# Linear attention into a Swish feed-forward layer: x of batches 1 and 2 transposed by DMA, loads issued behind it, num_mm of batch 2 earlier

## The chip, the cores and the metric

The kernel runs on one core of one Trainium2 chip. The metric is the device time of one launch in microseconds (us). The kernel before takes 293.0 us in the median of 13 runs (292.68 to 294.04). A core has a matmul engine (PE, with PEld for its weight loads), two engines for elementwise work (DVE and ACT), POOL (here mostly an issuer of loads), SP (here an issuer of stores and transposes) and 16 DMA engines[...].

## The reference, cut to what matters

```python
# q, k, v: [8 batches, 8 heads, 576 rows, 64]; w_in [512, 2048]; w_out [2048, 512]; beta [2048]
phi = lambda x: np.where(x > 0, x, np.exp(x) - 1.0) + 1.0
kv  = einsum('bhsd,bhse->bhde', phi(k), v)
num = einsum('bhsd,bhde->bhse', phi(q), kv)
den = einsum('bhsd,bhd->bhs', phi(q), phi(k).sum(axis=2)) + 1e-6
x   = (num / den).transpose(0, 2, 1, 3).reshape(4608, 512)
h   = x @ w_in
out = (h * sigmoid(beta * h)) @ w_out
```

## The kernel before, in words

The order on every engine is written by hand: instructions stand on each engine in the order in which the code calls them, and each waits for what it reads. Per batch of 576 rows there are four main tiles of 128 rows and a tail of 64; two tails together make one more tile, and the eight tails are handled as a ninth "batch" at the end.

A batch goes through these steps. `load_k`, `load_q` and `load_v` each issue two DMAs from POOL (L72 and L76), which turn float32 in memory into bf16 on chip. `exp_` (ACT, L229), `relu` (DVE, L237) and `phi` (DVE, L242) make phi of q and k; `v_copy` (DVE, L385) puts v beside columns of ones. `kv_mm` (PE, L362, 40 matmuls) and `kv_evac` (DVE, L372) make kv. q is transposed, in batch 1 by `q_trans` on PE (L395, with copies on ACT, L387), from batch 2 on by `q_trans_dma`, a DMA transpose on SP's queue (L407). `num_mm` (PE, L421, 4 matmuls a tile) and `num_norm` (DVE, L435 to L437) make a tile of x. x has to be transposed again to be the moving operand of the feed-forward layer. In batches 0 to 2 `x_trans` does that for the main tiles: 4 PE transposes (L455) and one copy on ACT or DVE (L385, L387). From batch 3 on, and for all tails, `num_norm` itself issues a DMA transpose on SP (L441); `by_dma` decides it with `DMA_T = 3`.

`h_phase` computes h by groups: a group is one block `ff` of 128 hidden units and a range of row tiles, 4 matmuls (L475) and one Silu on ACT (L467). `(ff, 0, 4)` is a full group, `(ff, 0, 2)` and `(ff, 2, 4)` are its halves, which can begin when only some tiles of x are there. `h_last` does the last four blocks of batches 0 and 1 in the PSUM buffer `att`, which has two slots. `y_phase_wide` (batches 0 and 1) runs over ff outside and the four tiles inside, and the last four ff tile by tile; `y_phase` (from batch 2 on) runs tile by tile. The matmuls of both are L527. `y_out` copies a result out (ACT L535 in the wide form, DVE L537 otherwise) and SP issues its store (L514 for batch 0, L519 for the others, L522 for the tails).

Attention of batch n+1 is threaded between the groups of batch n by a plan, a dictionary from group number to functions. The plan of `y_phase_wide` counts ff from 0 to 11 and then the four tiles as 12 to 15:

```python
y_phase_wide(1, {
    1: [F(phi, 2, 0), F(q_trans_dma, 2), F(phi, 2, 1)],
    6: [F(kv_mm, 2), F(kv_evac, 2), F(held_load, 4, 2)],
    11: [F(num_mm, 2, 0), F(num_norm, 2, 0)],
    12: [F(num_mm, 2, 1), F(num_norm, 2, 1), F(x_trans, 2, 0, wide=True, dve=True)],
```

Loads stand on POOL in the order k1, q1, w_out's third quarter (L111), v1, its fourth quarter, then k2, q2, v2, k3, q3, v3 without a wait for attention. `held_load` puts a one-element copy on POOL (`hold`, L598) that reads the end of a transposed q, so that all POOL issues behind it wait for that transpose.

Of the kernel before, what the change touches and what calls it, by code (L numbers as in the profile page):

```python
# [16 lines left out]
def kernel(  # L17
# [12 lines left out]
    B, H, S, D = q.shape  # L30
# [5 lines left out]
    NJ = 4  # L36
# [1 line left out]
    TAIL = S - MAIN  # L38
    NT = NJ + 1
    EA = D + 2  # L40
    DMA_T = 3
    TINY = 2.0 ** -30

    ctx.enter_context(tc.manual_schedule())
# [63 lines left out]
    def load_w_out(i):  # L108
        for ii in range(2):
            c0 = 4 * i + 2 * ii  # L110
            nc.gpsimd.dma_start(out=w_out_f[i][ii], in_=w_out_v[:, c0 : c0 + 2, :])  # L111
# [92 lines left out]
        nc.vector.tensor_add(beta_c, beta_s, beta_m)  # L204
        nc.vector.reciprocal(rbeta, beta_c)

    def w_out_scale(i, on_dve=4):
        for c in range(4):
            ff = 4 * i + c
            dst, src, by = w_out_sb[i][:, c, :], w_out_f[i][c // 2][:, c % 2, :], rbeta[:, ff : ff + 1]  # L210
            if c < on_dve:
                nc.vector.tensor_scalar(dst, src, by, None, ALU.mult)
            else:
                nc.scalar.activation(dst, src, ACTF.Copy, scale=by)  # L214
# [1 line left out]

    st = {}

    def by_dma(b):
        return b >= DMA_T  # L220

    def begin(b):
        st[b, "p"] = work.tile([P, 2, NT, DM], BF16, tag="qk_p", name="qk_p")
# [17 lines left out]
    def phi(b, a, h0=0, h1=H):  # L241
        nc.vector.tensor_tensor(  # L242
            st[b, "p"][:, a].rearrange("p j (h d) -> p h j d", h=H)[:, h0:h1],
            st[b, "r", a][:, h0:h1], st[b, "e", a][:, h0:h1], ALU.min,
        )
# [182 lines left out]
    def num_norm(b, t):  # L428
        n = P
        den = work.tile([P, 2, 4], F32, tag="den", name="den")  # L430
        rden = work.tile([P, 2, 4], F32, tag="rden", name="rden")
        xs = work.tile([P, 2, 4, D], BF16, tag="xs", name="xs", bufs=4)
        st[b, "xs", t] = xs
        nv = st[b, "n", t][:n, :, 0 : 4 * (D + 1)].rearrange("p a (h e) -> p a h e", h=4)
        nc.vector.tensor_scalar(den[:n], nv[:, :, :, D], 1e-6, None, ALU.add)  # L435
        nc.vector.reciprocal(rden[:n], den[:n])  # L436
        nc.vector.tensor_mul(  # L437
            xs[:n], nv[:, :, :, 0:D], rden[:n, :, :, None].to_broadcast([n, 2, 4, D])
        )
        if by_dma(b) or t == NJ:  # L440
            nc.sync.dma_start_transpose(  # L441
                out=x_dst(b, t), in_=xs.rearrange("p a h d -> p (a h d)")[:n]
            )
# [6 lines left out]
    def x_trans(b, t, wide=False, dve=False):  # L450
        n = P
        xv = st[b, "xs", t].rearrange("p a h d -> p (a h d)")
        tp = tr_bank(wide)[:, 0 : KC * P].rearrange("p (c n) -> p c n", c=KC)
        for p in range(KC):
            nc.tensor.matmul(  # L455
                tp[:, p, :n], xv[:n, p * P : (p + 1) * P], identity[:n, :n],
                is_transpose=True, start=True, stop=True, skip_group_check=True,
            )
        copy(x_dst(b, t), tp[:, :, :n], dve)
# [80 lines left out]
    def y_phase(b, plan):  # L540
        for t in range(4):
            if b == B and t == 3:
                y_end()
                return
            yp = mm_bank([P, DM])
            for ff in range(FC):
                y_mm(b, yp, t, ff)
                if ff % 4 == 3 and ff < FC - 1:
                    run(plan, 4 * t + ff // 4)
            y_out(b, t, yp)  # L550
            run(plan, 4 * t + 3)
# [33 lines left out]
    def load_next(b):
        if b < B:
            if b >= 5:
                load_v(b)
            load_k(b)
            load_q(b)  # L590
            if b < 5:
                load_v(b)

    held = consts.tile([1, 1], BF16)

    def hold(a):

        nc.gpsimd.tensor_copy(held, a)  # L598

    def held_load(b, n):  # L600

        hold(st[n, "qT"][0:1, NJ, KC - 1, 0:1])
        load_next(b)
# [12 lines left out]
    def F(f, *a, **k):  # L616
        return lambda: f(*a, **k)
# [31 lines left out]
    num_mm(0, 0)  # L649
    num_mm(0, 1)  # L650
    num_norm(0, 0)
    exp9(0, QF, N9)
    relu9(0, QF, N9)
    silu_table()
    warm(4)
    x_trans(0, 0, dve=True)
    num_norm(0, 1)
    phi9(0, QF, 6)
    phi9(0, 6, N9)
    qb2 = att_banks(BF16)  # L660


    load_w_out(2)
    load_v(1)
    load_w_out(3)

    def tidy():
# [3 lines left out]
    def q_rest():  # L671
        for t in range(2, NT):
            q_trans9(t, qb2, (t - 2) * 256)
        for t in range(2, NT):
# [5 lines left out]
        + [(ff, 0, 2) for ff in range(4, 8)] + [(ff, 2, 4) for ff in range(8)]  # L680
        + [(ff, 0, 4) for ff in range(8, 12)],
        {
            1: [F(x_trans, 0, 1)],
            3: [F(q_rest)],
            5: [F(num_mm, 0, 2), F(num_norm, 0, 2)],
            7: [F(num_mm, 0, 3), F(num_norm, 0, 3)],
# [5 lines left out]


    clear_tail(2)
    load_next(2)
    h_last(0, xT[0], [])
    begin(1)
    exp_(1, 1)
    exp_(1, 0)
    silu_table()  # L700
    relu(1, 1)
    relu(1, 0)
    w_out_scale(2)
    phi(1, 1)
    phi(1, 0)
    v_copy(1, 0, HH)
    v_copy(1, HH, H, dve=False)
    y_phase_wide(0, {
        4: [F(load_next, 3)],
        10: [  # L710
            F(q_trans, 1, 0, 1, 2, 3), F(kv_mm, 1), F(kv_evac, 1), F(w_out_scale, 3, 2),
        ],
        11: [F(num_mm, 1, 0), F(num_norm, 1, 0)],
        12: [F(num_mm, 1, 1), F(num_norm, 1, 1), F(x_trans, 1, 0, wide=True)],
        13: [F(num_mm, 1, 2), F(num_norm, 1, 2), F(x_trans, 1, 1, wide=True)],
        14: [F(num_mm, 1, 3), F(num_norm, 1, 3), F(q_trans, 1, 4)],
    })

    ALL = [(ff, 0, 4) for ff in range(FC)]
    h_phase(  # L720
        1, xT[1],
        [(ff, 0, 2) for ff in range(4)] + [(ff, 2, 4) for ff in range(4)] + ALL[4:12],
        {
            0: [F(x_trans, 1, 2), F(num_mm, 1, 4), F(num_norm, 1, 4)],
            1: [F(x_trans, 1, 3)],
            8: [F(begin, 2), F(relu, 2, 0)],
            10: [F(relu, 2, 1)],
            12: [F(v_copy, 2)],
        },
    )  # L730
    begin(3)
# [3 lines left out]
    silu_table()  # L735
    y_phase_wide(1, {
        1: [F(phi, 2, 0), F(q_trans_dma, 2), F(phi, 2, 1)],
        6: [F(kv_mm, 2), F(kv_evac, 2), F(held_load, 4, 2)],
        11: [F(num_mm, 2, 0), F(num_norm, 2, 0)],
        12: [F(num_mm, 2, 1), F(num_norm, 2, 1), F(x_trans, 2, 0, wide=True, dve=True)],  # L740
        13: [F(num_mm, 2, 2), F(num_norm, 2, 2)],
        14: [
            F(x_trans, 2, 1, wide=True, dve=True), F(num_mm, 2, 3), F(num_norm, 2, 3),
        ],
    })

# [61 lines left out]
```

## Time and profile before

| what | value |
|---|---|
| median of 13 runs | 293.0 us |
| the profiled execution's own time | 292.83 us |
| its span | 291.1 us |
| PE busy | 281.1 us |
| ACT busy | 173.4 us |
| DVE busy | 118.4 us |
| POOL busy | 50.9 us |
| first feed-forward matmul (L475) starts | 16.90 us |
| y_phase_wide of batch 0 starts | 33.33 us |
| h_phase of batch 1 starts | 51.53 us |
| h_last of batch 1 ends | 66.40 us |
| h_phase of batch 2 starts | 83.07 us |
| h_phase of batch 3 starts | 113.44 us |

Times in the profile count from the start of the span. The span is 1.73 us shorter than the profiled execution's time. The rows of stage starts come from the chain of work that ended last.

### The profile page before, as it was taken

To read this page: it belongs to the slowest core of one execution; us is meant where nothing else is said; L and a number is where in the kernel's file an instruction comes from. 1 tells how busy PE (TensorE), PEld (TensorE's weight loads), DVE (VectorE), ACT (ScalarE), POOL (GpSimd) and SP (SyncE) were. 2 spreads that over 40 slices of the span, in tenths; PEclk is the share of its full clock that TensorE was granted. 3 is DMA by queue.
4 is the path that set the end of the run, shared out by engine and by line. 5 is a ranking of instruction groups with operands and counts; after the bars stand their busy time and mean duration, and the time that the engine had idled before them with its cause. 6 is when DMAs were issued, how large, how long until landed. Compare 5 with 4: busy or idle time off the path is not lost.

```text
span 291.1 us, 4693 instructions
## 1 busy us (share of the span) xinstructions
PE 281.1 (97%) x1875; PEld 142.5 (49%) x1895; DVE 118.4 (41%) x239; ACT 173.4 (60%) x228; POOL 50.9 (17%) x73
## 2 busy tenths in 40 slices
PE   8779999999999999999999999999999999999994
PEld 3466455644574544445445444454445444444444
DVE  3874387504383275426441645173616400110012
ACT  2788798889987752876187718780760077017500
POOL 8924574100605000510041000000000000000000
PEclk9999999999999999999999999999999999999998
DMA  8999999995899984897279855032503400120033
GB/s 146 197 206 346 255 276 193 258 160 90 106 202 222 188 155 102 121 191 149 92 116 174 158 105 111 2 90 90 126 2 85 115 36 0 53 93 1 0 73 73
DMA packets 73590, 37.55 MB, mean 129 GB/s; under 512 B 41168, under 2 KB 68064, under 8 KB 73568
## 3 DMA queue, kind: packets, MB, share of 16 engines
q0 software_dynamic: 38912, 20.19, 48.5%
q1 hardware_dynamic: 34464, 16.92, 24.3%
q8 instruction: 15, 0.25, 0.3%
q10 hardware_dynamic: 192, 0.14, 0.2%
q14 instruction: 7, 0.06, 0.1%
HBM read 36.71 MB, written 9.44 MB: 159 GB/s over the span
## 4 chain that ended last, share of the span: by engine, by line
PE 91%; DMA 3%; POOL 3%; DVE 1%; issue 1%; ACT 1%; POOLq 0%
PE mm L475 41%; PE mm L527 41%; PE att L421 3%; DMA w_in<-in_moe_w_in_dram 3%; PE att L475 2%; PE att L362 2%; POOL xqk L135 1%; PE mm L559 1%; POOL vraw L135 1%; ACT q_pT L387 1%; PE mm L455 1%; DVE xs L437 0%; PE att L395 0%; PE att L455 0%; DVE xT L385 0%
## 5 line engine op out<-in xcount | busy, mean ns | idle before, releaser
L467 ACT ACTIVATE g<-mm,beta_c 128x512 bf16<-128x512 f32 (+2 forms) x156 | 97.2, 633 | 88.1 <-PE mm L475 87.9
L527 PE MATMUL mm<-w_out,g 128*128 128x512 bf16 x542 | 126.6, 379 | 1.2 <-issue 0.3
L475 PE MATMUL mm<-xT,w_in 128*128 128x512 bf16 (+2 forms) x560 | 107.9, 349 | 1.7 <-DMA w_in<-in_moe_w_in_dram 1.6
L475 PEld LDWEIGHTS <-w_in 128*128 128x128 bf16 x656 | 62.1, 98 | 62.7 <-DMA w_in<-in_moe_w_in_dram 1.8
L527 PEld LDWEIGHTS <-g 128*128 128x128 bf16 x560 | 53.1, 98 | 58.9 <-issue 0.3
L537 DVE COPY y_sb<-mm 128x512 f32<-128x512 f32 x27 | 18.7, 691 | 72.9 <-PE mm L527 69.4
L229 ACT ACTIVATE e<-xqk 128x2560 bf16<-128x2560 bf16 x14 | 31.9, 2329 | 0.1
L242 DVE TENSOR_TENSOR qk_p<-r,e 128x2560 bf16<-128x2560 bf16 x14 | 20.8, 1490 | 12.8 <-ACT e L229 12.1
L437 DVE TENSOR_TENSOR xs<-att,rden 128x512 bf16<-128x512 f32 x36 | 24.9, 691 | 1.2
L372 DVE CAST kv_bd<-att 64x260 bf16<-64x260 f32 x14 | 6.0, 427 | 33.0 <-PE att L362 32.9
L72 POOL DMA_DIRECT2D vraw<-in_v_dram x7 | 6.4, 916 | 65.6 <-DVE vaug L385 61.1
L435 DVE TENSOR_SCALAR den<-att 128x8 f32<-128x8 f32 x36 | 5.8, 162 | 29.5 <-PE att L421 29.4
L421 PEld LDWEIGHTS <-q_pT 128*128 128x128 bf16 (+1 forms) x160 | 10.7, 100 | 9.9 <-DVE xs L437 1.9
L421 PE MATMUL att<-kv_bd,q_pT 128*128 128x130 bf16 (+1 forms) x160 | 14.4, 222 | 0.9 <-ACT q_pT L387 0.5
L475 PE MATMUL mm<-xT_tail,w_in 128*128 128x512 bf16 x63 | 13.9, 379 | 0.1
L237 DVE TENSOR_SCALAR r<-xqk 128x2560 bf16<-128x2560 bf16 x14 | 11.4, 819 | 3.9 <-DMA xqk<-in_q_dram 2.4
L608 PE MATMUL mm<-g 128*128 128x512 bf16 x29 | 9.1, 470 | 1.3 <-DVE g L145 1.2
L229 ACT ACT_TABLE_LOAD x7 | 9.0, 1283 | 0.1
L436 DVE RECIPROCAL rden<-den 128x8 f32<-128x8 f32 x36 | 7.3, 203 | 1.2
L72 POOL DMA_DIRECT2D xqk<-in_k_dram x7 | 6.8, 972 | 3.8 <-DMA w_in<-in_moe_w_in_dram 2.4
L475 PE MATMUL att<-xT,w_in 128*128 128x512 bf16 x32 | 7.2, 379 | 0.0
L72 POOL DMA_DIRECT2D xqk<-in_q_dram x7 | 6.3, 902 | 3.9 <-ACT w_out L214 2.0
(77 smaller groups left out, 134.4 us busy)
## 6 DMA issues: line engine op xcount, KB each, us to landing
out_dram<-y_sb SPq DMA_DIRECT2D x28, 256.0 KB, 2.3
xqk<-in_k_dram POOLq DMA_DIRECT2D x7, 512.0 KB, 8.9
xqk<-in_q_dram POOLq DMA_DIRECT2D x7, 512.0 KB, 10.5
vraw<-in_v_dram POOLq DMA_DIRECT2D x7, 512.0 KB, 12.0
w_in<-in_moe_w_in_dram POOLq DMA_DIRECT2D x4, 512.0 KB, 10.1
g<-in_moe_w_out_dram POOLq DMA_DIRECT2D x4, 512.0 KB, 10.7
out_dram<-y_sb SPq DMA_DIRECT2D x14, 128.0 KB, 5.2
xqk<-in_moe_w_out_dram POOLq DMA_DIRECT2D x2, 512.0 KB, 13.8
```

The source lines that it names most:

```text
L72: eng.dma_start(out=dst[:, :, 0:NJ, :].rearrange("p h j d -> p h (j d)"), in_=src[b, :, 0:MAIN, :].rearrange("h (p j) d -> p h (j d)", j=NJ),)
L229: nc.scalar.activation(st[b, "e", a][:, h0:h1], xqk[b % NX][:, a, h0:h1], ACTF.Exp)
L237: nc.vector.tensor_scalar(st[b, "r", a][:, h0:h1], xqk[b % NX][:, a, h0:h1], 0.0, 1.0, ALU.max, ALU.add)
L242: nc.vector.tensor_tensor(st[b, "p"][:, a].rearrange("p j (h d) -> p h j d", h=H)[:, h0:h1], st[b, "r", a][:, h0:h1], st[b, "e", a][:, h0: ...
L421: nc.tensor.matmul(nps[r0 : r0 + n, p // 2, c0 : c0 + 2 * (D + 1)], st[bb, "qT"][:, t, p, :n], kv_bd[bb % 2][:, p], start=True, stop=True, ...
L436: nc.vector.reciprocal(rden[:n], den[:n])
L437: nc.vector.tensor_mul(xs[:n], nv[:, :, :, 0:D], rden[:n, :, :, None].to_broadcast([n, 2, 4, D]))
L467: nc.scalar.activation(g_sb[b % 2][:, ff, c0:c1], hp[:, c0:c1], ACTF.Silu, scale=beta_c[:, ff : ff + 1],)
L475: nc.tensor.matmul(hp[:, c0:c1], w_in_sb[ff // 4][:, kc, (ff % 4) * P : (ff % 4 + 1) * P], x[:, t0:t1, kc, :] if b < B else x[:, kc, c0:c1 ...
L527: nc.tensor.matmul(yp, g_sb[b % 2][:, ff, t * P : (t + 1) * P], w_out_sb[ff // 4][:, ff % 4, :], start=(ff == 0), stop=(ff == FC - 1),)
L537: nc.vector.tensor_copy(y_sb, yp)
L608: nc.tensor.matmul(st["warm"], g_sb[0][:, FC - 1, 0:P], g_sb[0][:, FC - 1, :], start=True, stop=True, skip_group_check=True,)
```

## The change

`DMA_T` goes, and `by_dma` sends the main tiles of every batch but 0 through the DMA transpose. With it go eight `x_trans` calls of batches 1 and 2. In batch 0, `x_trans` of tile 1 moves ahead of the first feed-forward group, and `num_norm` of tile 1 ahead of `exp9`. The first `load_v(1)` moves ahead of both halves of w_out's third quarter. The loads of batches 2 and 3 move behind a hold on x of batch 1, v3 behind a hold on batch 2's transposed q, k4 and q4 behind a hold on batch 2's x; in later batches v is loaded behind a hold on the transposed q in the middle of `h_phase`, and k and q behind a hold on x. `kv_mm` of batch 1 moves from step 10 to step 7 of its plan, and the `num_mm` calls of batch 2 from steps 11 to 14 to steps 8 to 11. Four more blocks of `h_phase` 1 and of `h_phase` 2 are halved. The scaling of w_out's last two quarters moves within the plan, six of its eight copies to ACT, and one Silu table load moves into the plan.

```diff
-    def by_dma(b):
-        return b >= DMA_T
+    def by_dma(b, t):
+        return b > 0 or t == NJ
...
-    def w_out_scale(i, on_dve=4):
-        for c in range(4):
+    def w_out_scale(i, cs=range(4), dve=True):
+        for c in cs:
...
+    def held_v(b, n):
         if b < B:
+            hold(st[n, "qT"][0:1, NJ, KC - 1, 0:1])
+            load_v(b)
+
+    def held_kq(b, n):
+        if b < B:
+            hold(xT[n % 3][0:1, NJ - 1, KC - 1, 0:1])
             load_k(b)
             load_q(b)
...
+    num_norm(0, 1)
     exp9(0, QF, N9)
     relu9(0, QF, N9)
+    warm(4)
+    x_trans(0, 0)
     silu_table()
-    warm(4)
-    x_trans(0, 0, dve=True)
-    num_norm(0, 1)
+    x_trans(0, 1, dve=True)
...
+    load_v(1)
     load_w_out(2)
-    load_v(1)
     load_w_out(3)
...
-            1: [F(x_trans, 0, 1)],
...
-    load_next(2)
     h_last(0, xT[0], [])
     begin(1)
     exp_(1, 1)
     exp_(1, 0)
-    silu_table()
     relu(1, 1)
     relu(1, 0)
-    w_out_scale(2)
     phi(1, 1)
+    v_copy(1)
     phi(1, 0)
-    v_copy(1, 0, HH)
-    v_copy(1, HH, H, dve=False)
     y_phase_wide(0, {
-        4: [F(load_next, 3)],
-        10: [
-            F(q_trans, 1, 0, 1, 2, 3), F(kv_mm, 1), F(kv_evac, 1), F(w_out_scale, 3, 2),
+        7: [
+            F(kv_mm, 1), F(w_out_scale, 2, (0, 1), False), F(q_trans, 1, 0, 1, 2, 3),
+            F(kv_evac, 1), F(w_out_scale, 2, (2, 3)),
         ],
-        11: [F(num_mm, 1, 0), F(num_norm, 1, 0)],
-        12: [F(num_mm, 1, 1), F(num_norm, 1, 1), F(x_trans, 1, 0, wide=True)],
-        13: [F(num_mm, 1, 2), F(num_norm, 1, 2), F(x_trans, 1, 1, wide=True)],
-        14: [F(num_mm, 1, 3), F(num_norm, 1, 3), F(q_trans, 1, 4)],
+        9: [F(num_mm, 1, 0), F(num_norm, 1, 0), F(w_out_scale, 3, range(4), False)],
+        10: [F(num_mm, 1, 1), F(num_norm, 1, 1)],
+        11: [F(num_mm, 1, 2), F(num_norm, 1, 2), F(silu_table)],
+        12: [F(num_mm, 1, 3), F(num_norm, 1, 3)],
+        13: [F(q_trans, 1, 4)],
     })
+    def load_late():
+        hold(xT[1][0:1, NJ - 1, KC - 1, 0:1])
+        for b in (2, 3):
+            load_k(b)
+            load_q(b)
+            if b == 2:
+                load_v(b)
...
-        [(ff, 0, 2) for ff in range(4)] + [(ff, 2, 4) for ff in range(4)] + ALL[4:12],
+        [(ff, 0, 2) for ff in range(8)] + [(ff, 2, 4) for ff in range(8)] + ALL[8:12],
         {
-            0: [F(x_trans, 1, 2), F(num_mm, 1, 4), F(num_norm, 1, 4)],
-            1: [F(x_trans, 1, 3)],
-            8: [F(begin, 2), F(relu, 2, 0)],
-            10: [F(relu, 2, 1)],
-            12: [F(v_copy, 2)],
+            0: [F(load_late), F(num_mm, 1, 4), F(num_norm, 1, 4)],
+            12: [F(begin, 2), F(relu, 2, 0)],
+            14: [F(relu, 2, 1)],
+            16: [F(v_copy, 2)],
         },
...
     y_phase_wide(1, {
         1: [F(phi, 2, 0), F(q_trans_dma, 2), F(phi, 2, 1)],
-        6: [F(kv_mm, 2), F(kv_evac, 2), F(held_load, 4, 2)],
-        11: [F(num_mm, 2, 0), F(num_norm, 2, 0)],
-        12: [F(num_mm, 2, 1), F(num_norm, 2, 1), F(x_trans, 2, 0, wide=True, dve=True)],
-        13: [F(num_mm, 2, 2), F(num_norm, 2, 2)],
-        14: [
-            F(x_trans, 2, 1, wide=True, dve=True), F(num_mm, 2, 3), F(num_norm, 2, 3),
-        ],
+        6: [F(kv_mm, 2), F(kv_evac, 2), F(held_v, 3, 2)],
+        8: [F(num_mm, 2, 0), F(num_norm, 2, 0)],
+        9: [F(num_mm, 2, 1), F(num_norm, 2, 1)],
+        10: [F(num_mm, 2, 2), F(num_norm, 2, 2)],
+        11: [F(num_mm, 2, 3), F(num_norm, 2, 3), F(held_kq, 4, 2)],
     })
...
-                [(ff, 0, 2) for ff in range(4)] + [(ff, 2, 4) for ff in range(4)] + ALL[4:]
+                [(ff, 0, 2) for ff in range(8)] + [(ff, 2, 4) for ff in range(8)] + ALL[8:]
             )
-            plan = {
-                0: [F(x_trans, 2, 2, dve=True)],
-                1: [F(x_trans, 2, 3, dve=True)],
-            }
...
-            plan[7 + o] = [F(v_copy, n)]
+            plan[7 + o] = [F(v_copy, n), F(held_v, n + 1, n)]
...
-        load_next(b + 3)
...
+            plan[12] = [F(held_kq, b + 3, n)]
```

More of the change, by code (lines that the diff above doesn't have):

```diff
@@ L40 @@
     EA = D + 2
-    DMA_T = 3
     TINY = 2.0 ** -30
@@ L205, in make_beta @@
         nc.vector.reciprocal(rbeta, beta_c)
-    def w_out_scale(i, on_dve=4):
-        for c in range(4):
+    def w_out_scale(i, cs=range(4), dve=True):
+        for c in cs:
             ff = 4 * i + c
             dst, src, by = w_out_sb[i][:, c, :], w_out_f[i][c // 2][:, c % 2, :], rbeta[:, ff : ff + 1]
-            if c < on_dve:
+            if dve:
                 nc.vector.tensor_scalar(dst, src, by, None, ALU.mult)
@@ L439, in num_norm @@
         )
-        if by_dma(b) or t == NJ:
+        if by_dma(b, t):
             nc.sync.dma_start_transpose(
@@ L583, in y_phase_wide @@
             run(plan, 12 + t)
[L585 to L592, printed above, removed]
     held = consts.tile([1, 1], BF16)
@@ L598, in hold @@
         nc.gpsimd.tensor_copy(held, a)
-    def held_load(b, n):
-        hold(st[n, "qT"][0:1, NJ, KC - 1, 0:1])
-        load_next(b)
+    def held_v(b, n):
[3 more added lines that the diff above has]
+    def held_kq(b, n):
+        if b < B:
+            hold(xT[n % 3][0:1, NJ - 1, KC - 1, 0:1])
+            load_k(b)
+            load_q(b)
     def warm(n):
@@ L699 @@
     exp_(1, 0)
-    silu_table()
     relu(1, 1)
     relu(1, 0)
-    w_out_scale(2)
     phi(1, 1)
+    v_copy(1)
     phi(1, 0)
-    v_copy(1, 0, HH)
-    v_copy(1, HH, H, dve=False)
     y_phase_wide(0, {
-        4: [F(load_next, 3)],
-        10: [
-            F(q_trans, 1, 0, 1, 2, 3), F(kv_mm, 1), F(kv_evac, 1), F(w_out_scale, 3, 2),
-        ],
-        11: [F(num_mm, 1, 0), F(num_norm, 1, 0)],
-        12: [F(num_mm, 1, 1), F(num_norm, 1, 1), F(x_trans, 1, 0, wide=True)],
-        13: [F(num_mm, 1, 2), F(num_norm, 1, 2), F(x_trans, 1, 1, wide=True)],
-        14: [F(num_mm, 1, 3), F(num_norm, 1, 3), F(q_trans, 1, 4)],
-    })
+        7: [
+            F(kv_mm, 1), F(w_out_scale, 2, (0, 1), False), F(q_trans, 1, 0, 1, 2, 3),
+            F(kv_evac, 1), F(w_out_scale, 2, (2, 3)),
+        ],
+        9: [F(num_mm, 1, 0), F(num_norm, 1, 0), F(w_out_scale, 3, range(4), False)],
[3 more added lines that the diff above has]
+        13: [F(q_trans, 1, 4)],
+    })
+    def load_late():
+        hold(xT[1][0:1, NJ - 1, KC - 1, 0:1])
+        for b in (2, 3):
+            load_k(b)
+            load_q(b)
+            if b == 2:
+                load_v(b)
     ALL = [(ff, 0, 4) for ff in range(FC)]
```

## Prediction

> **What bounds the kernel now.** I read the shares of busy time first, then the chain that ended last, then PE's busy time by stage.
>
> ```profile
> PE 281.1 (97%) x1875; PEld 142.5 (49%) x1895; DVE 118.4 (41%) x239; ACT 173.4 (60%) x228; POOL 50.9 (17%) x73
> ...
> PE 91%; DMA 3%; POOL 3%; DVE 1%; issue 1%; ACT 1%; POOLq 0%
> ```
>
> ```profile
> 16.90:33.30 16.40, 16.32 (x153) 11.09 (x154) 9.24 (x23) 12.69 (x29) 7.42 (x9) 1.00 1.27 264
> 33.30:51.50 18.20, 17.67 (x149) 9.38 (x149) 12.72 (x25) 16.04 (x18) 10.72 (x14) 1.00 1.43 251
> 51.50:66.40 14.90, 14.90 (x98) 8.49 (x96) 3.27 (x7) 13.07 (x21) 0.35 (x1) 1.00 1.44 202
> 66.40:83.00 16.60, 16.08 (x127) 8.18 (x128) 8.38 (x18) 15.65 (x15) 4.87 (x7) 1.00 0.85 114
> ```
>
> The columns after the stage are its length and the busy time of PE, PEld, DVE, ACT and POOL. PE waits for the first w_in block until 16.9 us and after that is nearly always at work, so only two things shorten the run: PE work taken away, or the few waits before 83 us. From 83 us on the chain holds no wait worth a tenth. The chain in order of time shows the pieces concerned:
>
> ```profile
> 22.27 0.43 DVE xT L385
> ...
> 78.33 0.70 DVE xs L437
> 79.03 0.05 issue
> 79.08 0.40 PE att L455 x4
> ...
> 83.51 0.22 PE mm L455 x4
> ```
>
> Four PE transposes of x take 0.22 us unhindered. Last, the timeline around batch 2's attention, since its inputs move:
>
> ```profile
> 64.99 4.56 ACT L229 ACTIVATE e<-xqk 128x2560 bf16<-128x2560 bf16 x2
> 67.36 1.49 DVE L242 TENSOR_TENSOR qk_p<-r,e 128x2560 bf16<-128x2560 bf16 x1 [11.41 <-ACT e L229]
> 68.91 3.07 SPq L407 DMA_TRANSPOSE q_pT<-qk_p  x1
> 73.81 0.18 POOL L598 COPY held<-q_pT 1x1 bf16<-1x1 bf16 x1 [21.96 <-DMA q_pT<-qk_p]
> 74.04 0.88 POOL L72 DMA_DIRECT2D xqk<-in_k_dram  x1
> ```
>
> Batch 2's exp, phi and transposed q follow each other closely, the transpose lands at 73.8, and num_mm uses it at 77.5. Its inputs came at 54 us or before, far ahead; that slack the change spends.
>
> [...]v2 has landed at 54.0 us (42.54 + 11.5), k3, next in the queue, only at 62.0 (44.27 + 17.7), because batch 0's stores and a tail transpose run between; without such company loads land 3.1 to 3.2 us apart. [...]here bytes begin to move 1.9 us after the issue at 74.04. [...]exp begins 0.02 us after the load of 63.69 to 64.97[...].
>
> **The change part by part**, as time on PE's path, against the profiled execution's 292.83 us (span 291.1 and 1.73 around it; the median of the runs is 293.0, 0.17 above).
>
> *Batch 0.* x_trans of tile 1 (0.23) moves ahead of 16.90, where PE waits for w_in anyway: its norm, now first on DVE, ends near 15.9, so the copy is done by 16.8. ACT loses a 0.60 copy between its Silus but starts them about 0.1 later, behind a table load that now ends near 17.4. x_trans of tile 3 then ends near 22.2, not 22.7, and ACT's Silus hold PE a little. I take -0.4 (0 to -0.55).
>
> *y_phase_wide 0* (33.33 to 51.53, 18.20 us). Two transposes leave: -0.44. Waits now: work is 64 x 0.2157 = 13.8, kv_mm 0.75, q_trans 1.13, num_mm 0.92, transposes 0.44, together 17.0, so 1.2 of wait. After: start 32.9, step 7 ends at 32.9 + 8 x 0.863 = 39.8; kv_mm waits for v_copy, which follows phi(1,1) and ends near 40.15 (0.35); q_trans waits for phi(1,0) until 41.65 (0.75). v1 lands near 38.5, one w_out quarter (2.6 us) sooner than its 41.4, since its two issues on POOL move past that quarter's two. The quarter itself comes near 41 and is scaled by 43.4, when ff 8 has just run; ff 10 needs that. w_out's last quarter on ACT (4 x 0.66 behind the q copies) ends near 47.2, as ff 15 begins. Waits about equal, so -0.4 in all (0 to -0.7); h_phase 1 starts at 50.75. The table load costs nothing: ACT ends it at 48.75, and y_out of the first tile (PE done at 47.6) has 2 us before its bank is wanted.
>
> *h_phase 1.* Two transposes leave (-0.44). Halved blocks: a half is 0.109 us a matmul, a full one 0.2157, so 16 x 0.003 = +0.05. A half's Silu takes 0.43 on ACT, PE's half 0.44: even. Its tile 3 is needed at 50.75 + 0.35 + 8 x 0.437 = 54.6. SP: three transposes (1.19 issue each), two stores (0.55 each), the fourth transpose at about 50.6, landing 2.4 later, 53.0. No wait (1.6 spare).
>
> *y_phase_wide 1 and h_phase 2.* Four transposes leave (-0.88), halves +0.05, and the 0.75 of waits (66.40 to 83.07 is 16.67; work 13.8 + 0.75 + 0.92 + 0.44 = 15.9) has no owner any more. The DMA transposes of x land 5 us and more before their use; SP queues four stores behind them, which nobody waits for soon. The eight ACT and DVE copies of x_trans (0.42 or 0.60 each) go too, off the path. The num_mm calls at steps 8 to 11 stand 1.1 us apart, and a num_norm takes 1.06 on DVE (0.17 + 0.20 + 0.69), so the two att slots come free in time.
>
> The sum so far: -0.4 - 0.4 - 0.39 - 0.83 - 0.75 = -2.8.
>
> *What the holds cost.* Before, POOL issued k2 at 35.8; now `hold` on x of batch 1 stops it, and k2, q2, v2, k3, q3 with it, until 53.0. k4 (issued 74.04) was whole at 80.7, q4 3.2 later. So alone: k2 at 53.3 + 6.7 = 60.0, q2 63.2, v2 66.3. Beside them run the last two or three of batch 0's eight stores and the tail transpose. That company cost 4.9 us (8.0 less 3.1) when all of it fell on loads; about a quarter falls here: +1.2, from 0 to 3. q2 64.4, v2 67.5.
>
> DVE has v_copy(2) ahead of phi(2,0): 67.5 + 0.85 + 1.49 = 69.85. q_trans_dma then takes 5.8 (the second one, which flew beside loads; 4.8 alone), as k3 and q3 are under way: 75.7. PE wants it after step 8: h_last ends at 66.4 - 1.2 = 65.2, plus 9 x 0.863 + 0.75 = 73.7. Wait 2.0. kv_mm's own wait lies inside that: exp of q and k, a table load and two Silus from 64.4 give an att slot at 71.55, wanted at 71.25. Each us more on v2 adds one. Bounds: 0 (alone 66.3 + 2.35 + 4.8 = 73.5) to 4.5.
>
> Behind it: exp(3) on ACT ends near 78.5 and y_out follows a table load later, in time for the first bank at 82. v3, now behind the transposed q, lands near 83, used at 90; k4 and q4 near 90 and 95, exp wants k4 at 98. Each hold is a POOL copy of 0.18 us on a queue with nothing but loads behind it, so its price is the delay of those loads alone. Later holds have still more room (k5 and q5 would come near 117, and exp wants k5 near 128), the order of SP's transposes and stores from batch 3 on is as before, and the later stages keep their length: 0.
>
> **Sum:** -2.8 + 2.0 = -0.8, from 292.83 to 292.0 us.
>
> **The rivals.**
> *Loads in time.* Stores have drained before the loads' bytes move, and the transposed q lands near 74. The wait is 0 to 1: 290.0 to 291.0, middle 290.4. For it: SP's own issue times; k4's first us moved little, so stores could use it. Against it: k3's 8 us behind v2.
>
> *Slower: batch 2's load chain.* v2 comes at 69.5 or later, since stores and the tail transpose cost their full share again and x of batch 1 releases the hold late. Everything from v_copy to num_mm(2,0) shifts; the point of balance is a wait of 2.8, that is v2 at 68.3, only 0.8 after my estimate. At v2 69.5 the wait is 4.0: 292.83 - 2.8 + 4.0 = 294.0.
>
> *The gain isn't there.* The transposes stood in holes that PE has anyway (waits on xs stay when they go), so 0.8 of the 1.76 comes back, and with a wait of 2: 292.8. Against it: in both h_phases no hole is seen.
>
> **How the numbers follow.** Likeliest (0.45): a wait of 1.2 to 2.8, 291.2 to 292.8, named 292.0. Loads in time 0.25, slower by the load chain 0.20, no gain 0.10. What a measurement of this kernel tells from no change is about 0.2%, 0.6 us, so faster means below 292.4: two thirds of the first case and all of the second, 0.55. Within: the rest of the first, most of the last, a little of the third, 0.24. Slower: 0.21. The range 290.2 to 293.8 leaves out a tenth on either side.
>
> **What would show it.** Right: first y_phase_wide near 32.9; h_phase 1 at 50.7 with no L455 of x after batch 0; POOL's hold released near 53; v_copy(2) waiting for v2 at 67.5; PE waiting about 2 us at num_mm(2,0) for the transposed q; h_phase 2 at 82.3; no other stage changed in length. Wrong: v2 before 66.5 or after 68.5, a wait of ACT's exp(3) on k3, or a new wait of PE in y_phase_wide 0.

## The result and the profile after

The changed kernel takes 297.29 us in the median of 7 runs (297.06 to 298.28); the kernel before takes 292.98 us in 32 runs (292.67 to 294.04). The ratio is 1.0151 with a 95% interval of 1.0140 to 1.0162: 4.3 us slower, where 292.0 was predicted. The profiled execution of the changed kernel took 296.71 us with a span of 294.6. It was the fastest of its eight executions: six of the other seven have a mean granted clock of 0.986 to 0.988 instead of 0.993, an estimated 3 us more at half clock ((0.993 - 0.988) x 295 / 0.5), and no trace shows where.

First the shares of busy time and the chain that ended last, as before the change:

```profile
PE 279.4 (95%) x1874; PEld 144.1 (49%) x1895; DVE 115.0 (39%) x231; ACT 174.5 (59%) x235; POOL 53.5 (18%) x82
...
PEclk9999999999799999999999999999999999999999
...
PE 70%; DMA 13%; issue 9%; POOL 4%; ACT 2%; DVE 1%; POOLq 0%; ACTq 0%
```

PE has less to do, as the change intends, and yet the span is longer. The chain now runs through DMA and issue for 22% of the span (4% before). In order of time it follows POOL's issues and a load of batch 1, then POOL's wait for the hold until 53.5 us (19.2 us, shown as issue), then q2's load (10.3 us), and comes back to PE only at `kv_mm` of batch 2. And in one slice, the eleventh, between 74 and 81 us, the granted TensorE clock is below full speed. Before the change it was so only in the last slice, behind the last matmul.

The same four stages as in the prediction, shifted to where they now begin (length, then busy time of PE, PEld, DVE, ACT and POOL, granted clock, DMA share, GB/s):

```profile
16.50:32.60 16.10, 15.95 (x148) 10.79 (x149) 8.63 (x22) 12.70 (x30) 6.81 (x9) 1.00 1.26 266
32.60:50.60 18.00, 16.82 (x138) 8.78 (x140) 11.16 (x21) 16.15 (x19) 1.72 (x2) 1.00 0.83 187
50.60:65.00 14.40, 14.38 (x105) 9.61 (x105) 1.06 (x3) 10.29 (x21) 8.03 (x11) 1.00 1.08 168
65.00:86.80 21.80, 16.98 (x118) 8.32 (x119) 12.85 (x22) 18.93 (x17) 1.75 (x3) 0.92 1.28 166
```

Only the last one, `y_phase_wide(1)`, is longer. From the first instruction of each stage in the timeline, in us:

| stage | before | after | difference |
|---|---|---|---|
| up to y_phase_wide 0 | 33.16 | 32.62 | -0.54 |
| y_phase_wide 0 | 18.21 | 18.00 | -0.21 |
| h_phase 1 and h_last | 14.87 | 14.35 | -0.52 |
| y_phase_wide 1 | 16.67 | 21.87 | +5.20 |
| h_phase 2 to the end | 208.2 | 207.8 | -0.4 |
| span | 291.1 | 294.6 | +3.5 |

(0.3 of the first difference is the first block of `w_in`, which landed at 16.53 here and at 16.85 in the execution of before.)

The timeline of the changed kernel from the hold to the first `num_mm` of batch 2 (start, duration, engine, line, operation; in brackets the idle time before it and what ended that; `x7` is a group of seven, with the time from the first one's start to the last one's end):

```profile
53.54 0.18 POOL L589 COPY held<-xT 1x1 bf16<-1x1 bf16 x1 [19.22 <-DMA xT<-xs]
54.02 0.89 POOL L71 DMA_DIRECT2D xqk<-in_k_dram  x1 [0.31 <-issue]
...
57.50 1.32 SPq L441 DMA_TRANSPOSE xT_tail<-xs  x1
...
66.78 1.28 ACT L229 ACT_TABLE_LOAD   x1 [4.38 <-DMA xqk<-in_q_dram]
...
68.07 4.56 ACT L229 ACTIVATE e<-xqk 128x2560 bf16<-128x2560 bf16 x2
...
72.00 4.01 SPq L407 DMA_TRANSPOSE q_pT<-qk_p  x1
72.66 1.28 ACT L467 ACT_TABLE_LOAD   x1
...
75.27 1.03 PE L362 MATMUL att<-vaug,qk_p 128*64 128x65 bf16 x40 [4.09 <-ACT g L467]
...
76.63 2.90 PE L527 MATMUL mm<-w_out,g 128*128 128x512 bf16 x7 [0.33 <-issue]
```

Read it from the top. The hold opens at 53.5, k2 is issued at 54.0, and q2 is whole at 66.7, which is when ACT can go on: it had been idle for 4.38 us. Only then does it load exp's table, then run two exps, load Silu's table and do the Silus of `h_last` that were queued behind. Those Silus free the `att` slot that `kv_mm(2)` needs, so PE stands still for 4.09 us ahead of L362. The seven matmuls that follow take 2.90 us, 0.41 each, instead of 0.216. The granted clock, microsecond by microsecond, says why (same columns as above):

```profile
74.00:75.00 1.00, 0.00 (x0) 0.11 (x1) 0.16 (x1) 1.00 (x2) 0.00 (x0) 1.00 1.84 188
75.00:76.00 1.00, 0.73 (x38) 0.73 (x38) 0.00 (x0) 1.00 (x3) 0.00 (x0) 0.84 1.24 219
76.00:77.00 1.00, 0.67 (x12) 0.44 (x8) 0.65 (x2) 0.98 (x2) 0.00 (x0) 0.50 1.27 290
77.00:78.00 1.00, 1.00 (x4) 0.39 (x3) 0.20 (x1) 0.99 (x2) 0.00 (x0) 0.50 0.43 94
78.00:79.00 1.00, 1.00 (x4) 0.37 (x3) 0.00 (x0) 1.00 (x1) 0.51 (x2) 0.50 0.08 16
79.00:80.00 1.00, 1.00 (x8) 0.53 (x7) 0.17 (x2) 1.00 (x2) 1.00 (x2) 0.95 0.00 0
```

By the PEclk column (0.84, three times 0.50, 0.95) the clock is half from 75.7 to 79.1, for 3.4 us, although PE is busy again from 75.3. So this wait cost more than its length: 4.09 for itself, 1.23 for the seven matmuls (2.90 less the 1.67 that they take at full clock in `e4_fill` below), 0.21 for `kv_mm` (1.03 against 0.82 there), and 0.33 of wait for x of batch 2 at the end. That is 5.86 of the 6.26 us by which this stage exceeds its undisturbed length of 15.61 (the kernel `e7_batch2` below).

### The profile page after: what moved, and what is told of

The parts are those of the page before. It is cut to its first block, busy times and chain, and to the rows that moved or that the text cites. A ratio compares the mean times of both kernels' runs of the same rounds, so it can differ in the third digit from the quotient of the medians.

```text
span 294.6 us, 4739 instructions
## 1 busy us (share of the span) xinstructions
PE 279.4 (95%) x1874; PEld 144.1 (49%) x1895; DVE 115.0 (39%) x231; ACT 174.5 (59%) x235; POOL 53.5 (18%) x82
## 4 chain that ended last, share of the span: by engine, by line
PE 70%; DMA 13%; issue 9%; POOL 4%; ACT 2%; DVE 1%; POOLq 0%; ACTq 0%
PE mm L475 33%; PE mm L527 33%; DMA xqk<-in_k_dram 5%; DMA xqk<-in_q_dram 3%; DMA w_in<-in_moe_w_in_dram 3%; PE att L421 2%; PE att L362 2%; DMA xT<-xs 2%; POOL xqk L134 1%; PE mm L559 1%; POOL vraw L134 1%; ACT e L229 1%; POOL g L110 1%; POOL xqk L71 1%; DVE xs L437 0%
## 5 line engine op out<-in xcount | busy, mean ns | idle before, releaser
L467 ACT ACTIVATE g<-mm,beta_c 128x512 bf16<-128x512 f32 (+2 forms) x164 | 98.5, 614 | 86.1 <-PE mm L475 85.8
L475 PEld LDWEIGHTS <-w_in 128*128 128x128 bf16 x688 | 65.3, 98 | 59.2 <-DMA w_in<-in_moe_w_in_dram 0.8
L237 DVE TENSOR_SCALAR r<-xqk 128x2560 bf16<-128x2560 bf16 x14 | 11.5, 825 | 17.8 <-DMA xqk<-in_q_dram 16.3
L589 POOL COPY held<-xT 1x1 bf16<-1x1 bf16 x5 | 1.9, 373 | 63.9 <-DMA xT<-xs 63.9
L589 POOL COPY held<-q_pT 1x1 bf16<-1x1 bf16 x5 | 0.9, 176 | 56.4 <-DMA q_pT<-qk_p 56.4
L362 PE MATMUL att<-vaug,qk_p 128*64 128x65 bf16 x280 | 6.0, 199 | 4.4 <-ACT g L467 4.1
L606 PE MATMUL mm<-g 128*128 128x512 bf16 x29 | 8.3, 436 | 1.3 <-DVE g L144 1.2
L362 PEld LDWEIGHTS <-qk_p 128*64 128x64 bf16 x280 | 5.3, 113 | 7.5 <-DVE qk_p L242 3.5
```

The lines of the kernel that those rows point to most:

```text
L237: nc.vector.tensor_scalar(st[b, "r", a][:, h0:h1], xqk[b % NX][:, a, h0:h1], 0.0, 1.0, ALU.max, ALU.add)
L362: nc.tensor.matmul(kvp[g * D : (g + 1) * D, p, :], st[b, "p"][:, 1, j, c0 : c0 + D], vaug[b % 2][:, j, 2 * p + g, 0 : D + 1], start=(j == ...
L467: nc.scalar.activation(g_sb[b % 2][:, ff, c0:c1], hp[:, c0:c1], ACTF.Silu, scale=beta_c[:, ff : ff + 1],)
L475: nc.tensor.matmul(hp[:, c0:c1], w_in_sb[ff // 4][:, kc, (ff % 4) * P : (ff % 4 + 1) * P], x[:, t0:t1, kc, :] if b < B else x[:, kc, c0:c1 ...
L606: nc.tensor.matmul(st["warm"], g_sb[0][:, FC - 1, 0:P], g_sb[0][:, FC - 1, :], start=True, stop=True, skip_group_check=True,)
```

## The experiments

Two theories stood at the start. *The load chain*: the hold makes batch 2's k, q and v late, so that the change would pay if they came early. *The transposes*: the DMA transposes of x need quiet queues, the hold is what gives them that, and early loads would only move the wait to x. All medians below are compared with the kernel before on the same chip.

**e1_nohold: the changed kernel with the loads early.**

```diff
     clear_tail(2)
+
+    def load_late():
+        for b in (2, 3):
...
+    load_late()
...
-    def load_late():
-        hold(xT[1][0:1, NJ - 1, KC - 1, 0:1])
...
-            0: [F(load_late), F(num_mm, 1, 4), F(num_norm, 1, 4)],
+            0: [F(num_mm, 1, 4), F(num_norm, 1, 4)],
```

> The changed kernel with one thing undone: batch 2's and 3's k, q and v are issued straight behind w_out's last quarter, with no hold on x of batch 1. Theory (the late loads of batch 2 stop ACT at exp, so that the att slots come free late and PE stands still before kv_mm(2), then runs at half clock for some us): q2 and v2 are there before 56, PE waits under 0.5 us at kv_mm(2), the clock stays at 1.0, and about 6 us go: 290.5 to 291.5. Rival (x by DMA transpose is what costs, as its transposes now share the DMA engines with loads): x of batch 1 lands late, PE waits at the second halves of h_phase 1, and no more than 2 us go: 295 or more.

Measured: 298.90 us (297.43 to 299.87), ratio 1.0194 (1.0158 to 1.0231). The load chain as the only cause has fallen; the second theory said this. The wait of `kv_mm(2)` is gone and `y_phase_wide(1)` takes 16.2 us, but PE now stands ahead of `h_phase(1)`. First the four transposes of x of batch 1 in the changed kernel (the last column is the median time from issue to landing, in us), then the same line in this experiment:

```profile
xT<-xs SPq DMA_TRANSPOSE x4, 2.5
```

```profile
xT<-xs SPq DMA_TRANSPOSE x4, 8.1
```

And what PE waits for here, as the waits and the timeline of the experiment show it (total, times, longest):

```profile
PE mm L475 <- DMA xT<-xs: 5.0, 2, 4.6
```

```profile
56.61 1.01 PE L475 MATMUL mm<-xT,w_in 128*128 128x256 bf16 x4 [4.59 <-DMA xT<-xs]
```

Beside a queue full of loads a tile of x takes 8.1 us instead of 2.5, and the wait has moved 19 us upstream with much the same length: 4.6 instead of 4.1. Here too the clock is half, from 55.7 to 62.5. This profile also has a half clock from 18.1 to 21.6, which the changed kernel's has not, and `h_phase(0)` takes 17.2 us with it instead of 16.05. So 1.1 us of this execution have nothing to do with the transposes; the mean clock of the four runs (0.983, 0.982, 0.988, 0.988) suggests that two of them had such a stretch.

**e10_early2: only k3 and q3 held.** k2, q2 and v2 go early, as few loads as the change could need.

```diff
+    load_k(2)
+    load_q(2)
+    load_v(2)
...
         hold(xT[1][0:1, NJ - 1, KC - 1, 0:1])
-        for b in (2, 3):
...
+        load_k(3)
+        load_q(3)
```

> The changed kernel with k2, q2 and v2 issued early, behind w_out's last quarter, and only k3 and q3 behind the hold on x of batch 1. Theory (a DMA transpose of x lands about 2.5 us after its issue alone and 7 to 8 us after it beside a filled load queue, so either the loads or the transposes come late): batch 2's exp no longer waits, but x of batch 1 lands 1 to 3 us after PE wants it, PE waits ahead of h_phase 1 and its clock may fall: 293 to 296. Rival (only the loads' lateness cost time): 290 to 291.5.

Measured: 298.36 us (297.88 to 299.0), ratio 1.0175 (1.0153 to 1.0197). The transposes land 7.4 us after their issue in the median, and the wait ahead of `h_phase(1)` is 4.3 us. Three loads are enough for the whole effect, and the middle that I expected isn't there.

**e2_tile0: the hold opens at the first tile of x, not at the fourth.**

```diff
-        hold(xT[1][0:1, NJ - 1, KC - 1, 0:1])
+        hold(xT[1][0:1, 0, KC - 1, 0:1])
```

> The changed kernel with the hold of batch 2's loads on tile 0 of batch 1's x instead of tile 3; tile 0 lands about 5 us sooner (near 48.3 against 53.5). Theory of the late loads: everything on that chain comes up to 5 us sooner, q2 near 61.5 and v2 near 64.5, so the wait of 4.1 us at kv_mm(2) is all but gone and the clock with it: 290.5 to 292. Rival (the DMA transposes of x themselves): they now meet loads, tile 3 lands later, and nothing is won: 297.

Measured: 299.52 us (297.9 to 301.57), ratio 1.0223 (1.016 to 1.0287). The hold opens at 48.2, over 5 us sooner, but the transpose of tile 3, issued at 50.9, now takes 8.4 us; PE waits 4.7 us at 59.3, in the middle of `h_phase(1)`, and works at half clock until 63.6. Opening the hold sooner trades one wait for the other.

**e5_holdonly: the kernel before, with the loads held.** x of batch 1 stays on PE, and so the loads have no DMA transpose of a main tile beside them.

```diff
-    load_next(2)
...
-        4: [F(load_next, 3)],
...
+    def load_late():
+        hold(xT[1][0:1, NJ - 1, KC - 1, 0:1])
+        for b in (2, 3):
+            load_next(b)
...
-            1: [F(x_trans, 1, 3)],
+            1: [F(x_trans, 1, 3), F(load_late)],
```

> The kernel before with one part of the change: batch 2's and 3's loads stand behind a hold on tile 3 of batch 1's x (made by PE transposes there), all else as before. Theory (late loads alone stop ACT and PE; the DMA transposes of x are not needed for it): kv_mm(2) waits 2 to 4 us for an att slot, the clock falls to a half for some 3 us after it, and the run takes 296 to 299. Rival (the cost comes with the DMA transposes of x): 293 to 294.

Measured: 301.08 us (299.48 to 302.54), ratio 1.0294 (1.0268 to 1.032). Holding the loads costs more than I gave it, even without the other parts of the change. Here v3 is in the queue as well, and batch 2's transposed q runs beside k3, q3 and v3. The DMA lines of the kernel before and of this one:

```profile
q_pT<-qk_p SPq DMA_TRANSPOSE x1, 4.8
```

```profile
q_pT<-qk_p SPq DMA_TRANSPOSE x1, 11.1
```

```profile
PE att L421 <- DMA q_pT<-qk_p: 4.1, 2, 2.8
...
PE att L362 <- ACT g L467: 1.1, 1, 1.1
```

The first line is two waits, one for batch 2 and one for batch 3:

```profile
81.34 0.61 PE L421 MATMUL att<-kv_bd,q_pT 128*128 128x130 bf16 x4 [2.85 <-DMA q_pT<-qk_p]
106.41 0.41 PE L421 MATMUL att<-kv_bd,q_pT 128*128 128x130 bf16 x4 [1.25 <-DMA q_pT<-qk_p]
```

The wait of 2.85 stands where the prediction had put one, at `num_mm(2,0)`; around it the clock is half from 81.3 to 84.7. The transposed q was issued only 1.3 later than in the kernel before (70.20 against 68.91) and landed 7.5 later, so most of this wait is again a DMA transpose beside loads, and less of it the lateness of the loads themselves.

**e11_pe1: the changed kernel with all four loads early and batch 1's x on PE.** Both conflicts are taken away; what is left of the change is the start, the new order in `y_phase_wide(0)`, batch 2's part and the later holds.

```diff
-        return b > 0 or t == NJ
+        return b > 1 or t == NJ
...
     clear_tail(2)
...
+    load_late()
...
-        12: [F(num_mm, 1, 3), F(num_norm, 1, 3)],
-        13: [F(q_trans, 1, 4)],
+        12: [F(num_mm, 1, 3), F(num_norm, 1, 3), F(x_trans, 1, 0, wide=True, dve=True)],
+        13: [F(x_trans, 1, 1, wide=True, dve=True)],
+        14: [F(q_trans, 1, 4)],
...
-        hold(xT[1][0:1, NJ - 1, KC - 1, 0:1])
...
-            0: [F(load_late), F(num_mm, 1, 4), F(num_norm, 1, 4)],
+            0: [F(x_trans, 1, 2), F(num_mm, 1, 4), F(num_norm, 1, 4)],
+            1: [F(x_trans, 1, 3)],
```

> The changed kernel with all loads of batches 2 and 3 early and batch 1's x transposed on PE again; start, step 7 for kv_mm(1) and batch 2's x by DMA as in the change. Theory (the two conflicts between loads and transposes are gone, nothing else in the change costs time): like the version with batch 2's part alone, 291 to 292.2. Rival (another part, the start or the earlier kv_mm(1), costs too): 292.8 or more.

Measured: 292.65 us (292.13 to 296.19), ratio 0.9995 (0.9981 to 1.001). That gives back the whole loss, 4.6 us from 297.29. With `e1_nohold`, which differs only in who transposes x of batch 1, the pair is clean: with the same early loads, PE transposes give 292.65 and DMA transposes 298.90. It comes out above the range of the theory (to 292.2) and just under that of the rival (from 292.8), by which another part of the change costs time too. So that rival isn't excluded: 0.4 us of wait on x of batch 2 remains, and `y_phase_wide(0)` takes 18.75 us here, 18.21 before.

| k, q, v of batch 2 and k, q of 3 | x of batch 1 on PE | x of batch 1 by DMA |
|---|---|---|
| early | 292.65 (e11_pe1) | 298.90 (e1_nohold) |
| held until x of batch 1 is there | 301.08 (e5_holdonly, else as before, v3 held too) | 297.29 (the change) |

**e7_batch2: the kernel before up to h_phase 1, the changed one from there.** Batch 2's `num_mm` at steps 8 to 11, its x by DMA, k4 and q4 behind it, the halves in `h_phase(2)` and all later holds.

```diff
-    DMA_T = 3
+    DMA_T = 2
...
-        6: [F(kv_mm, 2), F(kv_evac, 2), F(held_load, 4, 2)],
...
+        6: [F(kv_mm, 2), F(kv_evac, 2)],
+        8: [F(num_mm, 2, 0), F(num_norm, 2, 0)],
...
+        11: [F(num_mm, 2, 3), F(num_norm, 2, 3), F(held_kq, 4, 2)],
...
-                [(ff, 0, 2) for ff in range(4)] + [(ff, 2, 4) for ff in range(4)] + ALL[4:]
+                [(ff, 0, 2) for ff in range(8)] + [(ff, 2, 4) for ff in range(8)] + ALL[8:]
...
+            plan[12] = [F(held_kq, b + 3, n)]
```

> The kernel before up to the end of h_phase 1 (batch 1's x on PE, early loads), and the change from there on: batch 2's num_mm at steps 8 to 11, its x by DMA with no load beside it, k4 and q4 behind it, more halves in h_phase 2, later loads as in the change. Theory (a DMA transpose of x costs PE nothing where no loads run beside it and num_mm is early enough): y_phase_wide 1 and h_phase 2 lose the 0.88 of transposes and most of 0.75 of waits, 291.3 to 292.2. Rival (the DMA transposes of x are late in any case): a wait ahead of h_phase 2 and 293 or more.

Measured: 292.04 us (291.6 to 293.27, 22 runs) against 292.91, ratio 0.9969 (0.9961 to 0.9977). This is the only version that beats both kernels. Its `y_phase_wide(1)` and the transposes of x in it:

```profile
66.20:81.80 15.60, 15.60 (x122) 7.80 (x121) 10.02 (x18) 15.51 (x15) 0.00 (x0) 1.00 0.39 74
```

```profile
xT<-xs SPq DMA_TRANSPOSE x4, 2.4
```

PE is busy throughout the stage, the DMA engines carry 74 GB/s (166 in the changed kernel), and each transpose lands in 2.4 us. With quiet queues the idea works.

**e9_start: the kernel before with the changed order in batch 0.**

```diff
     num_norm(0, 0)
+    num_norm(0, 1)
...
-    silu_table()
...
-    x_trans(0, 0, dve=True)
-    num_norm(0, 1)
+    x_trans(0, 0)
+    silu_table()
+    x_trans(0, 1, dve=True)
...
-            1: [F(x_trans, 0, 1)],
```

> The kernel before with the change's order at the start of batch 0 alone: norm and transpose of tile 1 ahead of the first feed-forward group. Theory of the prediction: 0.3 to 0.5 us less, 292.4 to 292.6. Rival (PE has more holes ahead of w_in now, and in some executions the clock falls to a half near 18 us for 3 us, as seen in two of the profiles of the experiments): a part of the runs 1 to 1.5 us longer, the median at 293 to 294.

Measured: 292.94 us (292.62 to 293.31), ratio 0.9995 (0.9983 to 1.0006). Nothing that can be measured. In its profile `y_phase_wide(0)` begins 0.5 sooner and then takes 18.79 us instead of 18.21, so that what the start gains is lost again one stage later.

**e8_tail: the changed kernel with batch 1's tail tile of x transposed on PE.** One long DMA transpose less beside batch 2's loads (it took 8.5 us there).

```diff
-        return b > 0 or t == NJ
+        return (b, t) != (1, NJ) and (b > 0 or t == NJ)
...
+            5: [F(x_trans, 1, NJ)],
```

> The changed kernel with batch 1's tail tile transposed on PE (0.22 us) instead of by the DMA that took 8.5 us beside k2 and q2. Theory (stores and that transpose take time from the loads of batch 2): q2 lands 1 to 1.5 us sooner than 66.7, kv_mm(2) waits 2.6 to 3.1 us, 295 to 296.3. Rival (the loads run at their own pace): 297.

Measured: 296.99 us (295.25 to 297.87 in 4 runs), ratio 1.0131 (1.0099 to 1.0162). As a time it is inconclusive, since its runs spread over 2.6 us and include the changed kernel's. The trace, of the execution with 295.25, agrees with the mechanism: q2 lands 11.3 us after k2's issue instead of 12.7, and the wait of `kv_mm(2)` is 2.5 instead of 4.1. Part of that comes back as 0.7 of wait ahead of `h_phase(2)`, and the clock is half from 73.6 to 77 all the same.

**e3_table: exp's table loaded ahead of q2**, by an Exp of one element, which changes no output.

```diff
+    def exp_table():
+        nc.scalar.activation(small[:, 1:2], small[:, 0:1], ACTF.Exp)
...
-    h_last(1, xT[1], [F(exp_, 2, 0), F(exp_, 2, 1)])
+    h_last(1, xT[1], [F(exp_table), F(exp_, 2, 0), F(exp_, 2, 1)])
```

> The changed kernel with a one-element Exp on ACT ahead of exp(2,0), so that the table load no longer waits for q2 together with the first exp. Theory: 1.3 us less on the chain from q2 to the att slot; PE's wait at kv_mm(2) falls from 4.1 to about 2.8 us, and if the half clock comes from the length of that wait it may shrink or go too: 294.3 to 296. Rival (v2, phi and the transposed q set the end of the wait, not ACT): no change, 297.

Measured: 299.25 us (298.48 to 300.08), ratio 1.0207 (1.0176 to 1.0238). The wait that it aimed at fell by 1.7, but the time did not fall with it. The waits of PE in this kernel:

```profile
PE att L362 <- ACT g L467: 2.4, 1, 2.4
PE mm L475 <- DMA xT<-xs: 2.2, 1, 2.2
PE att L421 <- DMA q_pT<-qk_p: 1.6, 1, 1.6
```

The two lower ones are new: the transposed q takes 7.7 us here, and the transposes of x of batch 2 take 7.1 to 4.5, so DMA ends last again. (1.1 us of this profile belong to a half clock from 17.6 to 21.0, before anything that was edited.)

**e4_fill: matmuls with a zero matrix in the wait.** Eighteen matmuls add zeros to an open sum ahead of `kv_mm(2)` and leave the result as it is; PE isn't idle there, so the clock should stay.

```diff
...
+    def fill(n):
+        for _ in range(n):
+            nc.tensor.matmul(
+                st["yp"][3], zeros[:, 0:P], zeros,
+                start=False, stop=False, skip_group_check=True,
+            )
...
-        6: [F(kv_mm, 2), F(kv_evac, 2), F(held_v, 3, 2)],
+        6: [F(fill, 18), F(kv_mm, 2), F(kv_evac, 2), F(held_v, 3, 2)],
```

> The changed kernel with 18 matmuls of zeros (128x512) that add nothing to an output bank, ahead of kv_mm(2), to fill PE's wait of 4.1 us. Theory (the clock falls because PE stands still): the wait stays but the clock stays at 1.0 and the matmuls after it take 0.216 and not 0.41 us: 1.5 to 2 us less, 295.3 to 296. Rival (the slow stretch has another cause, or the 18 matmuls stand in the path): 297 or more.

Measured: 300.57 us (300.1 to 300.79), ratio 1.0253 (1.0235 to 1.0271). The clock part is confirmed in the timeline; the gain is not, as the waits show:

```profile
71.40 4.05 PE L615 MATMUL mm<-zeros 128*128 128x512 bf16 x18
...
76.36 1.67 PE L528 MATMUL mm<-w_out,g 128*128 128x512 bf16 x7 [0.16 <-issue]
```

```profile
PE mm L476 <- DMA xT<-xs: 2.2, 1, 2.2
PE att L422 <- DMA q_pT<-qk_p: 1.8, 1, 1.8
```

The same seven matmuls take 1.67 us instead of 2.90: the slow matmuls in the changed kernel are the idle time's doing. But what they cost was cover for the transposed q, which lands 7.7 us after its issue here; PE waits for that and then for x of batch 2 (7.0 to 4.4 us a tile beside v3's load), and there the clock falls after all, from 90.0 to 93.4. Neither repair paid, with the DMA transposes still beside loads. Why the transposed q took 7.7 in this profile and in `e3_table`'s, and 6.0 in the changed kernel's, stays open; in all three k3 and q3 were still under way.

## Why the prediction was wrong

Stage by stage the gain came nearly as forecast; the price of the hold is what was wrong. By the prediction's own steps:

- *Batch 0, -0.4.* Not confirmed: the profile shows -0.54, of which 0.3 is a sooner `w_in`, and the order done alone has a ratio of 0.9995 (`e9_start`), where -0.4 would be 0.9986, inside its interval but at the edge.
- *y_phase_wide 0, -0.4.* -0.21: half.
- *h_phase 1, -0.39.* -0.52. The stage has no wait in the changed kernel, and its transposes of x land in 2.5 us as reckoned. That rests on the hold: with loads beside them they cost 4.3 to 4.7 of wait (`e1_nohold`, `e10_early2`, `e2_tile0`). The prediction gave the hold a price and never asked what it shields.
- *y_phase_wide 1 and h_phase 2, -0.83 and -0.75.* Right, stage by stage, in `e7_batch2`, where nothing comes late: 15.61 against 16.67 for the first, -1.06. `h_phase(2)` takes 14.75 against 15.16 there and in the changed kernel, -0.41. Together -1.47 against -1.58; as a whole kernel `e7_batch2` gains 1.05 between the profiled executions and 0.87 in the median. All five steps make -2.74 (with `y_phase_wide(1)` from `e7_batch2`), where the prediction has -2.8; that includes the 0.3 of `w_in`, which was luck.
- *Later holds, 0.* Right: every stage after `h_phase(2)` has its old length within 0.03.
- *What the holds cost: "Wait 2.0".* This is the step that failed: the stage lost 6.26 against its undisturbed length. Its path was wrong, the term for the loads was too small, that for the transposed q was right here but too narrow in its bounds, and two were missing, exp's table load and the clock:
  - *Place of the wait.* The prediction followed v2 to the transposed q and `num_mm(2,0)` and said of the other path "kv_mm's own wait lies inside that", with the att slot at 71.55. PE waited on that other path, from q2 through ACT to `kv_mm(2)`, and the slot came at 75.27. 2.3 of these 3.7 are q2; 1.28 are exp's table load: the prediction's sum has one table load, Silu's. Exp's stands behind the same wait as the first exp and starts only when q2 is there (66.78); `e3_table` took 1.7 off the wait by forcing it forward.
  - *Loads.* "+1.2, from 0 to 3" for company. Reckoned from the issue at 54.02, q2 alone would be whole 9.9 us later (6.7 for k2 and 3.2 more), at 63.9; it was whole at 66.7, so company cost 2.8. `e8_tail` puts 1.4 of it on the tail's transpose. The hold opened 0.5 late, and k2's issue was 0.7 late. Together q2 came 2.3 after the 64.4 of the prediction, v2, at 69.4, 1.9 after its 67.5, past the 68.5 that it had named as a sign of being wrong.
  - *Transposed q.* 6.0 against 5.8, right here. It landed at 78.0, and PE, held up at `kv_mm(2)`, came for it only at 79.4. Without that wait PE would have been there at 73.7 (an estimate: 71.18 + 0.82 + 1.67), 4.3 too soon. So both paths were some 4 us late, and mending one leaves the other, as `e3_table` and `e4_fill` show. It took 7.7 there and 11.1 in `e5_holdonly`. The 5.8 was a single case from the trace, and the range should have allowed for more.
  - *The clock.* Nothing was charged for what a wait does to PE afterwards: 1.23 + 0.21 here. In the changed kernel the clock was half (0.50) for 3.4 us after the wait of 4.09; it was half for 3.4 us after waits of 2.22 us (`e4_fill`, 90.0 to 93.4) and 2.49 us (`e8_tail`, 73.6 to 77.0) too, so these shorter waits were no protection. (After a wait of 2.23 us in `e3_table` the clock stayed whole; the last section shows it.)

The rival "batch 2's load chain" had late loads as the cause, and with v2 at 69.5 a wait of 4.0; v2 came at 69.4 and PE waited 4.09. The size agrees by luck, since that rival too had the wait at `num_mm(2,0)` and not at `kv_mm(2)`. Of the 2.7 between its 294.0 and the 296.71 of the profiled execution, 1.4 are the clock, for which it had nothing.

One reading in the prediction is off, and no term rests on it: by the packets of the trace, bytes begin to move 1.6 us after the issue at 74.04 (the first packet of that queue starts at 75.65), not 1.9.

That DMA transposes and loads are what collide is shown by the pair of `e11_pe1` (292.65 us) and `e1_nohold` (298.90), and by the landing times (2.5 us for a tile of x of batch 1 in the changed kernel, 8.1 in `e1_nohold`). By what mechanism they slow each other down wasn't tried, and no run here shows it.

## What to carry to other kernels

Moving a transpose from PE to DMA saved PE 0.22 us a tile here, but bought a deadline in the DMA queues: count what is under way at that moment, since a tile took 2.5 us in quiet queues (the changed kernel) and 7.0 to 8.4 beside a queue of loads (`e1_nohold`), and holding the loads back to keep the queues quiet only turned the delay over to whoever needed the loads (4.09 us of PE at `kv_mm(2)`). Ask of every hold what it delays and also what it protects, and follow the delay through every engine to its end, table loads included. And price a PE wait with the slow matmuls that may follow it: they cost some 1.4 us after the one of 4.1 us here, and the clock fell after waits from 2.2 us up.

## What the runs showed of the hardware

- A DMA transpose of one tile of x (128 rows by 512) landed 2.4 us (`e7_batch2`) to 2.5 us (batch 1 in the changed kernel) after its issue alone, 3.6 to 5.1 us beside one load (the first three of batch 2 in the changed kernel, beside v3; 5.4 to 7.1 at the same place in `e3_table` and `e4_fill`), 7.0 to 8.4 us beside a queue of loads (`e1_nohold`). That of q for a batch took 4.8 alone (the kernel before and `e7_batch2`), 6.0 (the changed kernel) to 7.7 (`e3_table`, `e4_fill`) beside k3 and q3, 11.1 beside k3, q3 and v3 (`e5_holdonly`), 11.9 for batch 3 in the changed kernel, beside k4, q4 and four stores.
- Loads came later too: q2 was whole 12.7 us after k2's issue beside stores and one tail transpose (the changed kernel), 11.3 without the transpose (`e8_tail`).
- In the traces here the changes of the granted clock lay whole multiples of 3.41 us apart: in the changed kernel at 75.68, 79.09 and 294.13 (1 and 63 times 3.413), in `e1_nohold` the two falls at 18.14 and 55.70 (11 times), in `e3_table` at 17.62 and 75.64 (17 times), in `e4_fill` at 11.54 and 90.04 (23 times). From 22 us to the last matmul it fell from full to half in eight of the profiles, once in each, and each time at the end of a step of this grid in which PE had stood idle for 2.2 us or more: 3.00 us in the changed kernel, 2.49 in `e8_tail`, 2.22 in `e4_fill` and, the least, 2.18 in `e2_tile0`. No step with that much idle time was followed by one at full clock, and 1.77 us (`e4_fill`, 76.4 to 79.8) was not enough. So in these runs it mattered how a wait lay on the grid. In `e4_fill` a wait of 2.22 us lay inside one step (length and busy time of PE first, PEclk third from the end), and the next step is at half clock:

```profile
86.63:90.04 3.41, 1.18 (x9) 0.75 (x9) 3.38 (x4) 0.93 (x3) 0.00 (x0) 1.00 1.34 233
90.04:93.45 3.41, 3.41 (x19) 2.35 (x17) 0.02 (x1) 2.20 (x5) 2.67 (x5) 0.50 1.07 279
```

In `e3_table` a wait of 2.23 us, from 87.67 to 89.90, was divided between two steps, and the clock stayed whole:

```profile
85.88:89.29 3.41, 1.73 (x8) 0.58 (x6) 3.27 (x4) 1.79 (x3) 0.00 (x0) 1.00 1.42 159
89.29:92.70 3.41, 2.80 (x26) 2.55 (x27) 1.42 (x2) 2.17 (x5) 1.24 (x3) 1.00 1.12 336
```

- The fall came with the end of the step and not with the wait: 2.2 us (`e2_tile0`) to 4.5 us (the changed kernel and `e10_early2`) after the wait's beginning. In the changed kernel it hit work that had resumed 0.4 us before. It lasted one step (3.4 us, as in the changed kernel) or two (6.8 us, `e1_nohold` and `e2_tile0`). Before 22 us it was less simple: in `e4_fill` the clock fell at 11.5 after a step with 0.9 to 1.0 us idle, in `e1_nohold` and `e3_table` at 18.1 and 17.6 after one with 1.5 to 1.7, while in the kernel before a step with 1.46 us idle (12.86 to 16.27) left it whole.
